# A VectorE division queued behind the activation of the tile at which it is emitted

## The chip, the cores and the metric

The kernel runs on one core of one Trainium2 chip. Its time is the device time of one execution in microseconds (us); lower is better. Three runs of the kernel before the change took 780.65 to 781.32 us, with a median of 781.09 us. The profile is one execution of the same program, recorded by the hardware profiler.

## The reference

Three stages follow one another (batch 4, 8 heads, 768 positions, head size 64; 3072 tokens of 512 values):

```
scores = [ q.k within 16 positions , q.(max of k over each 32) + log 32 ] / sqrt(64)
a      = exp(scores - rowmax);  a = a / (sum(a) + 1e-9)
x      = a @ [v ; mean of v over each 32]          # attention, reshaped to 3072 x 512
h      = x @ w_in;  x = (h * cos(h)) @ w_out       # 512 -> 2048 -> 512
logits = x @ phi;  d = softmax over tokens;  c = softmax over the 32 slots
out    = c @ experts(d.T @ x)                      # 8 experts, 4 slots each
```

The line that matters here is the division `a / (sum(a) + 1e-9)`.

## The kernel before

**Middle stage.** The 3072 tokens are taken in 6 blocks of 512, and the 2048 hidden values in 16 slices of 128, so there are 96 tiles `s`, 16 to a block. For each tile TensorE makes `h` with 12 matmuls of 512 columns (`mm1`: L384, L385, L388; the operands are split in a high and a low part). VectorE rounds in two steps (`act1`: L402, L403), ScalarE takes the sine (L404), VectorE multiplies by `h` (`act2`: L409), ScalarE makes the high part (L412) and GpSimd the low one (L413). Two tiles later TensorE adds the product to four accumulators with 12 more matmuls (`mm2`: L425, L426, L429). `h` has two PSUM buffers, so `mm1` of tile s + 2 needs that L409 of tile s is done. At the end of a block the accumulators are copied to `x` by VectorE (L448, two of them) and ScalarE (L446, two), and the next block's first `mm2` waits for these copies. The weights of each tile are split by ScalarE (L372) and GpSimd (L373).

**Attention inside the tiles.** The attention of a later block runs between these tiles. It is cut into 24 groups `g`, and from group 8 on two groups make a pair that shares one tile `S` of 128 x 16 x 120 values. Per pair and in this order: scores on TensorE (L286), scale and mask (L290), row maximum (L298) and its subtraction (L302) on VectorE, one exponential for both groups on ScalarE (L307), then for each group the row sum (L312), and the division in three VectorE instructions (`att_norm`: L326 adds 1e-9 and a factor on 128 x 8, L328 takes the reciprocal, L329 multiplies 128 x 960 values). TensorE then transposes the group in two halves (`att_C`: L336) and multiplies by v (`att_D`: L354). There are 8 pairs from group 8 on; the first is groups 8 and 9, the last groups 22 and 23.

**What sets the order.** The calls are entered under half tiles (`at2`) and emitted by `fire` while the tile loop runs: position 0 of a tile lies between its `act1` and its `act2`. The division of the first group of a pair is emitted at half tile n, that of the second at n + 4, so two tiles later: at tiles 17 and 19 for the first pair, 25 and 27 for the next, and so on in steps of 8 up to 73 and 75. The first transposition of a group is emitted one tile after its division. From tile 17 on (`MAN0`) the queues of TensorE and of the DMA-issuing engine hold their work in the order of emission. VectorE, ScalarE and GpSimd are ordered by a planner (`schedule_with_timeline_sim`), which takes what is ready first in its own simulated time; it may run an instruction well ahead of where it was emitted.

Of the kernel before, what the change touches and what calls it, by code (L numbers as in the profile page):

```python
# [15 lines left out]
ALU = mybir.AluOpType  # L16
# [58 lines left out]
MAGIC = 12582912.0  # L75
# [3 lines left out]
def body(ctx: ExitStack, tc: tile.TileContext, q0, qk, kT, vn, vx, w, phi, ex, cst, out):  # L79
    nc = tc.nc  # L80
# [241 lines left out]
    def att_norm(g, eng=None):  # L322

        d = grp[g]
        sm = d["sm"]
        nc.vector.tensor_scalar(out=sm, in0=sm, scalar1=1e-9, scalar2=W_SCALE * TWO_PI, op0=ALU.add, op1=ALU.mult)  # L326
        rs = stat.tile([128, 8], F32, name=f"rs{g}", tag="rs")
        nc.vector.reciprocal(out=rs, in_=sm)  # L328
        (eng or nc.vector).tensor_tensor(out=d["S"], in0=d["S"],  # L329
                                         in1=rs.unsqueeze(2).to_broadcast([128, 8, KC]), op=ALU.mult)  # L330
# [47 lines left out]
    def mm1(s):  # L378
# [9 lines left out]
            nc.tensor.matmul(h, lo[:, c], xh[s // NF][:, t, :], start=False, stop=t == 3)  # L388
        hps[s] = h

    def act1(s):
        h = hps[s]
        a = ring.tile([128, TB], F32, name=f"a{s}", tag="a")
        if s < NACT:
            nc.scalar.activation(a, h, AF.Identity, bias=magic)
            nc.vector.scalar_tensor_tensor(out=a, in0=a, scalar=MAGIC, in1=h, op0=ALU.subtract, op1=ALU.subtract)
            if s < NABS:
                nc.scalar.activation(a, a, AF.Abs)
            else:
                nc.vector.tensor_single_scalar(out=a.bitcast(I32), in_=a.bitcast(I32), scalar=0x7FFFFFFF, op=ALU.bitwise_and)  # L400
        else:
            nc.vector.tensor_scalar(out=a, in0=h, scalar1=0.25, scalar2=MAGIC, op0=ALU.add, op1=ALU.add)  # L402
            nc.vector.scalar_tensor_tensor(out=a, in0=a, scalar=MAGIC, in1=h, op0=ALU.subtract, op1=ALU.subtract)  # L403
        nc.scalar.activation(a, a, AF.Sin, bias=halfpi, scale=-TWO_PI)  # L404
        gs[s] = a

# [131 lines left out]
    def at(s, pos, fn, *a):  # L538
        bg.setdefault((s, pos), []).append((fn, a))

    def at2(h, fn, *a):
        at(max(h, 0) // 2, max(h, 0) % 2, fn, *a)
# [51 lines left out]
    for token in PRE.split():  # L594
        n = token.lstrip("FfIMNASPKQWBVGXmksevtdcwa")
        todo[token[:len(token) - len(n)]](int(n or 0))


    for g in range(4, 24):
        h0 = HF[g // 2 % 2] + 2 * NF * (g // 4 - 1) if g > 7 else HB[g // 2 % 2]  # L600
        h = h0 + OA * (g % 2)
        n = h0 + ON + DN * (g % 2)
        if g < 8:
            if g > 5:
                at2(h - OV, load_v, g)
                at2(h - OV + 1, load_vs, g)
                at2(h - OK, att_K, g)
            c = n + OC
            at2(c + OD, att_D, g)
        else:  # L610
            v = n - 14 + OD2
            at2(v + 1, load_v, g)
            at2(v + 2, load_vs, g)
            at2(h - OK, att_K, g)
            c = n + OC2
            at2(n + OD2, att_D, g)
        at2(h, att_A, g)
        if g < 8:
            at2(h + 1, att_max, g, True)
            at2(h0 + OX, att_exps, g)  # L620
        else:
            at2(h + 1, att_max, g)
            at2(h + 1, att_sub, g)
            if g % 2:
                at2(h0 + OX, att_exp, g // 2)
            at2(h0 + OS + 2 * (g % 2), att_sum, g)
        at2(n, att_norm, g)
        at2(c, att_C, g, 0)
        at2(c + 1, att_C, g, 1)
        if g + 2 < 24:  # L630
            at2(h0 + OQ if g < 8 else h + 1, load_qk, g + 2)
# [48 lines left out]
    for s in range(NSLOT + LAG):  # L680
        if MAN is not None and s == MAN0:
            guard = tc.manual_schedule(engines=MAN)
            guard.__enter__()
        if s < NSLOT:
            mm1(s)
        if s + 1 < NSLOT:
            split_w((s + 1) % NF, 0, nc.vector if s + 1 < NF else None)
        if 0 <= s - LAG + 1 < NSLOT:
            split_w((s - LAG + 1) % NF, 1)
        if s < NSLOT:  # L690
            act1(s)
        fire(s, 0)
        if s < NSLOT:
            act2(s)
        if s >= LAG:
            mm2(s - LAG)
            if (s - LAG) % NF == NF - 1:
                last = [x2_out(t) for t in range(4)][3]
        fire(s, 1)
        fire(s, 2)  # L700
        if s - LAG >= NSLOT - NF:
            grab(wres, f"w{s - LAG - (NSLOT - NF)}")
# [66 lines left out]
    for k in range(4):  # L769
# [3 lines left out]
                                    in1=rz.unsqueeze(1).to_broadcast([128, 4, 32]), op=ALU.mult)  # L773
# [170 lines left out]
```

## Time and profile before

| | |
|---|---|
| timed, median of 3 | 781.09 us (780.65 to 781.32) |
| profiled execution, first to last instruction (span) | 778.9 us |
| its own time outside the span | not listed; the span is 2.19 us under the median of the timed runs |
| TensorE matmul busy | 740.2 us (95%) |
| VectorE busy | 473.6 us (61%) |
| ScalarE busy | 433.4 us (56%) |
| GpSimd busy | 428.6 us (55%) |
| chain that ended last, by engine | PE 63%, DVE 13%, ACT 12%, DMA 6% |

PE is TensorE, PEld its weight load, DVE VectorE, ACT ScalarE, POOL GpSimd, SP the engine that issues DMAs. Times are us from the start of the span. In a row of the timeline the first number is the start, the second the duration; `x4` means four such instructions in a row; what stands in brackets is how long the engine had been idle and what ended that idle time. The modelled ends of matmuls overlap the next start, so the distance between starts tells more of TensorE's pace than the duration.

### The profile page before, as it was taken

How to read it: one execution, taken by the hardware profiler on the slowest of the kernel's cores; microseconds unless marked ns; L12 is line 12 of the kernel's file. 1: busy time of each engine (PE TensorE's matmuls, PEld its weight loads, DVE VectorE, ACT ScalarE, POOL GpSimd, SP SyncE). 2: the span in 40 equal slices, each digit the busy share in tenths (PEclk: the TensorE clock that was granted, in tenths of full speed). 3: DMA queues.
4: the chain of work that ended last, by engine and by line, in shares of the span. 5: the costliest groups of instructions: out<-in, count | busy, mean ns of one | idle time of the engine just before them, and what ended most of it. 6: DMA issues, size and time to landing. Idle time of an engine off the chain costs nothing.

```text
span 778.9 us, 13853 instructions
## 1 busy us (share of the span) xinstructions
PE 740.2 (95%) x5517; PEld 573.5 (74%) x5517; DVE 473.6 (61%) x686; ACT 433.4 (56%) x786; POOL 428.6 (55%) x302
## 2 busy tenths in 40 slices
PE   9977799998999999998999999999999999999994
PEld 7866678776877787776787777778768888786453
DVE  4578896767477576576575684774773444433523
ACT  4979868636465455574465555464554455443222
POOL 2555884365557657556566566665576665752000
PEclk9997999999999999999999999999999999999998
DMA  9988753121120331311211211301101922328978
GB/s 331 396 264 331 271 164 113 42 97 59 48 95 1 100 105 29 121 68 41 87 44 33 72 40 33 111 0 35 33 1 56 392 93 82 109 81 299 371 306 268
DMA packets 35585, 101.69 MB, mean 131 GB/s; under 512 B 3393, under 2 KB 13889, under 8 KB 33473
## 3 DMA queue, kind: packets, MB, share of 16 engines
q1 hardware_dynamic: 35520, 100.81, 36.8%
q8 instruction: 43, 0.70, 0.4%
q14 instruction: 22, 0.17, 0.1%
HBM read 92.54 MB, written 6.29 MB: 127 GB/s over the span
## 4 chain that ended last, share of the span: by engine, by line
PE 63%; DVE 13%; ACT 12%; DMA 6%; issue 4%; SPq 0%; ACTq 0%; DVEq 0%
PE acc L425 8%; PE h L384 8%; PE acc L426 8%; PE h L385 8%; PE acc L429 7%; PE h L388 7%; PE av L354 3%; DVE S L329 2%; DMA qk<-in_qk_dram 2%; PE yp L842 2%; DMA kr<-in_kT_dram 2%; PE sc L286 2%; PE hp L809 2%; ACT a L404 2%; DVE a L403 2%
## 5 line engine op out<-in xcount | busy, mean ns | idle before, releaser
L373 POOL TENSOR_TENSOR wol<-w,woh 128x512 fp32r<-128x512 f32 x96 | 143.9, 1500 | 115.0 <-ACT woh L372 115.0
L413 POOL TENSOR_TENSOR gl<-a,gh 128x512 fp32r<-128x512 f32 x96 | 129.0, 1343 | 83.8 <-ACT gh L412 78.3
L384 PE MATMUL h<-xh,wih 128*128 128x512 f32 x384 | 156.4, 407 | 6.7 <-DVE a L409 6.6
L425 PE MATMUL acc<-woh,gh 128*128 128x512 f32 x384 | 157.4, 410 | 3.5 <-DVE x L448 3.5
L385 PE MATMUL h<-xl,wih 128*128 128x512 f32 x384 | 152.2, 396 | 0.0
L426 PE MATMUL acc<-wol,gh 128*128 128x512 f32 x384 | 152.1, 397 | 0.0
L373 POOL TENSOR_TENSOR wil<-w,wih 128x512 fp32r<-128x512 f32 x81 | 113.9, 1406 | 42.8 <-PE h L388 24.2
L402 DVE TENSOR_SCALAR a<-h 128x512 f32<-128x512 f32 x96 | 65.9, 686 | 115.8 <-PE h L388 110.7
L404 ACT ACTIVATE a<-a,halfpi 128x512 f32<-128x512 f32 x96 | 69.4, 724 | 115.7 <-DVE a L403 115.4
L388 PE MATMUL h<-xh,wil 128*128 128x512 f32 x384 | 104.9, 395 | 0.0
L429 PE MATMUL acc<-woh,gl 128*128 128x512 f32 x384 | 104.6, 393 | 0.0
L409 DVE TENSOR_TENSOR a<-h,a 128x512 f32<-128x512 f32 x96 | 66.1, 689 | 57.0 <-ACT a L404 56.9
L425 PEld LDWEIGHTS acc<-woh,gh 128*128 128x128 f32 x384 | 72.4, 188 | 28.6 <-issue 11.8
L384 PEld LDWEIGHTS h<-xh,wih 128*128 128x128 f32 x384 | 72.7, 189 | 24.6 <-DVE a L409 8.4
L372 ACT CAST wih<-w 128x512 fp32r<-128x512 f32 x96 | 59.2, 617 | 47.2 <-PE h L385 46.4
L388 PEld LDWEIGHTS h<-xh,wil 128*128 128x128 f32 x384 | 72.5, 189 | 16.3 <-issue 0.2
L429 PEld LDWEIGHTS acc<-woh,gl 128*128 128x128 f32 x384 | 72.1, 189 | 16.4 <-issue 0.6
L385 PEld LDWEIGHTS h<-xl,wih 128*128 128x128 f32 x384 | 72.8, 190 | 15.2 <-issue 0.3
L426 PEld LDWEIGHTS acc<-wol,gh 128*128 128x128 f32 x384 | 72.6, 189 | 14.6 <-issue 0.6
L412 ACT CAST gh<-a 128x512 fp32r<-128x512 f32 x96 | 59.3, 619 | 32.8 <-DVE a L409 32.8
L372 ACT CAST woh<-w 128x512 fp32r<-128x512 f32 x96 | 59.1, 616 | 21.7 <-PE acc L429 20.8
L403 DVE SCALAR_TENSOR_TENSOR a<-a,h 128x512 f32<-128x512 f32 x96 | 65.5, 683 | 2.1
(137 smaller groups left out, 945.8 us busy)
## 6 DMA issues: line engine op xcount, KB each, us to landing
ex<-in_ex_dram SPq DMA_DIRECT2D x64, 512.0 KB
raw<-in_w_dram SPq DMA_DIRECT2D x16, 1024.0 KB
qk<-in_qk_dram SPq DMA_DIRECT2D x20, 736.0 KB
v<-in_vx_dram SPq DMA_DIRECT2D x24, 512.0 KB
kr<-in_kT_dram SPq DMA_DIRECT2D x16, 384.0 KB
vb<-in_vn_dram SPq DMA_DIRECT2D x12, 512.0 KB
out_dram<-o SPq DMA_DIRECT2D x12, 512.0 KB
v<-vs SPq DMA_DIRECT2D x40, 48.0 KB
```

The lines of the kernel that those rows point to most:

```text
L372: nc.scalar.copy(hi, W[f][:, part, :])
L373: (eng or nc.gpsimd).tensor_tensor(out=lo, in0=W[f][:, part, :], in1=hi, op=ALU.subtract)
L384: nc.tensor.matmul(h, hi[:, c], xh[s // NF][:, t, :], start=t == 0, stop=False)
L385: nc.tensor.matmul(h, hi[:, c], xl[s // NF][:, t, :], start=False, stop=False)
L388: nc.tensor.matmul(h, lo[:, c], xh[s // NF][:, t, :], start=False, stop=t == 3)
L403: nc.vector.scalar_tensor_tensor(out=a, in0=a, scalar=MAGIC, in1=h, op0=ALU.subtract, op1=ALU.subtract)
L404: nc.scalar.activation(a, a, AF.Sin, bias=halfpi, scale=-TWO_PI)
L409: nc.vector.tensor_tensor(out=a, in0=h, in1=a, op=ALU.mult)
L413: nc.gpsimd.tensor_tensor(out=gl, in0=a, in1=gh, op=ALU.subtract)
L425: nc.tensor.matmul(acc[t], gh[:, c], hi, start=f == 0, stop=False)
L426: nc.tensor.matmul(acc[t], gh[:, c], lo, start=False, stop=False)
L429: nc.tensor.matmul(acc[t], gl[:, c], hi, start=False, stop=f == NF - 1)
```

## The change

A call of `act1` now keeps its L403 instruction, and the division of the second group of a pair, from group 9 on, is emitted inside `tc.issue_after(...)` of the latest one. That adds, to each VectorE instruction traced in the block, an edge by which it stands behind that L403 in VectorE's queue. No instruction, buffer or semaphore's meaning is added or taken away; the division of the first group and of groups below 8 is emitted as before.

```diff
+    turn_dve = {}
+
     def act1(s):
...
-            nc.vector.scalar_tensor_tensor(out=a, in0=a, scalar=MAGIC, in1=h, op0=ALU.subtract, op1=ALU.subtract)
+            turn_dve["a"] = nc.vector.scalar_tensor_tensor(out=a, in0=a, scalar=MAGIC, in1=h, op0=ALU.subtract, op1=ALU.subtract)
...
+    def later(g):
+        with tc.issue_after(turn_dve["a"].ins):
+            att_norm(g)
...
-        at2(n, att_norm, g)
+        at2(n, att_norm if g < 8 or g % 2 == 0 else later, g)
```

## Rows read from the trace of the kernel before

**Rows 1.** Windows: stretch, length, busy per engine, then granted clock, DMA share, GB/s
```profile
176.00:600.00 424.00, 411.95 (x2850) 324.06 (x2850) 278.05 (x393) 238.04 (x386) 259.51 (x183) 1.00 0.17 54
600.00:690.00 90.00, 90.00 (x449) 72.43 (x446) 37.96 (x62) 44.22 (x74) 58.54 (x46) 1.00 0.43 158
```

**Rows 2.** Waits of PE from 176 to 600: who for whom, us, times, longest
```profile
PE h L384 <- DVE a L409: 4.8, 4, 1.4
PE acc L425 <- DVE x L448: 3.5, 3, 1.3
PE vs L184 <- DVE d L501: 1.8, 1, 1.8
PE tr L336 <- ACT aT L342: 0.2, 1, 0.2
```

**Rows 3.** Timeline of DVE around the pair of groups 10 and 11
```profile
241.39 4.25 DVE L329 TENSOR_TENSOR S<-S,rs 128x960 f32<-128x960 f32 x2
245.57 0.68 DVE L402 TENSOR_SCALAR a<-h 128x512 f32<-128x512 f32 x1
...
247.83 0.69 DVE L409 TENSOR_TENSOR a<-h,a 128x512 f32<-128x512 f32 x1 [0.79 <-ACT a L404]
```

**Rows 4.** Timeline of PE, where it waits for DVE in three pairs
```profile
183.35 0.50 PE L384 MATMUL h<-xh,wih 128*128 128x512 f32 x1 [1.38 <-DVE a L409]
...
248.58 0.50 PE L384 MATMUL h<-xh,wih 128*128 128x512 f32 x1 [1.15 <-DVE a L409]
...
297.12 0.60 PE L336 MATMUL tr<-ident,S 128*120 128x128 f32 x4
...
298.98 0.47 PE L425 MATMUL acc<-woh,gh 128*128 128x512 f32 x1 [1.26 <-DVE x L448]
```

**Rows 5.** Timeline of PE without such a wait, tile 28
```profile
258.52 1.08 PE L388 MATMUL h<-xh,wil 128*128 128x512 f32 x4
259.43 0.60 PE L336 MATMUL tr<-ident,S 128*120 128x128 f32 x4
259.79 0.48 PE L425 MATMUL acc<-woh,gh 128*128 128x512 f32 x1
```

**Rows 6.** Timeline of PE at the first transposition of group 18
```profile
463.78 1.08 PE L388 MATMUL h<-xh,wil 128*128 128x512 f32 x4
...
464.98 0.63 PE L336 MATMUL tr<-ident,S 128*120 128x128 f32 x4
```

**Rows 7.** Timeline of DVE around the pair of groups 12 and 13
```profile
295.71 1.66 DVE L329 TENSOR_TENSOR S<-S,rs 128x960 f32<-128x960 f32 x1
297.29 0.94 DVE L170 TENSOR_REDUCE ks<-kr 128x24 f32<-128x768 f32 x1
298.15 1.27 DVE L448 TENSOR_SCALAR x<-acc 128x512 f32<-128x512 f32 x2
```

**Rows 8.** The division's lines on DVE: count, ns min/median/max, first and last start
```profile
L326 DVE TENSOR_SCALAR sm<-sm x24: 154/164/1285, 18.0 to 570.7; 128x8 f32<-128x8 f32 x24
...
L328 DVE RECIPROCAL rs<-sm x24: 144/202/205, 18.2 to 572.0; 128x8 f32<-128x8 f32 x24
...
L329 DVE TENSOR_TENSOR S<-S,rs x20: 1150/2079/2254, 62.1 to 574.2; 128x960 f32<-128x960 f32 x20
```

**Rows 9.** Timeline of POOL beside the division of groups 10 and 11
```profile
242.43 2.21 POOL L373 TENSOR_TENSOR wil<-w,wih 128x512 fp32r<-128x512 f32 x1
```

**Rows 10.** Timeline of DVE at tile 27, where group 11's division is emitted
```profile
252.45 0.69 DVE L403 SCALAR_TENSOR_TENSOR a<-a,h 128x512 f32<-128x512 f32 x1
...
257.31 0.69 DVE L363 TENSOR_TENSOR xl<-av,xh 128x512 fp32r<-128x512 f32 x1 [2.63 <-ACT xh L362]
259.71 0.69 DVE L402 TENSOR_SCALAR a<-h 128x512 f32<-128x512 f32 x1 [1.71 <-PE h L388]
```

**Rows 11.** Timeline of DVE and then PE at tiles 67 and 68, group 21
```profile
528.35 0.68 DVE L403 SCALAR_TENSOR_TENSOR a<-a,h 128x512 f32<-128x512 f32 x1
...
534.58 0.60 PE L336 MATMUL tr<-ident,S 128*120 128x128 f32 x4
```

## The prediction

> **What bounds the kernel now.** I read four views. First the page's busy shares: TensorE's is by far the largest, VectorE's the next. Then the windows, to see whether that share hides idle places: from 600 to 690 us TensorE is busy 90.00 of 90.00 us, while in the stretch with the interleaved attention, 176 to 600 us, it is busy 411.95 of 424 us; the granted clock is 1.00, the higher of its two levels, 2.4 GHz, in both [rows 1]. So 12 us of that stretch are idle, and TensorE is at a full clock even where it never pauses. Third, the list of TensorE's waits in that stretch, which names what ends them: four waits for the multiplication L409, three for the accumulator copies L448, one for L501 and one for an ACT copy [rows 2]. The only other one of size is that of a transposition for its own group's division, in the first pair; it is the first group's, so it stays. Last, the timeline of VectorE ahead of one such wait: before it, both divisions of the pair run back to back, 4.25 us for the two L329, and the rounding L402 of the next tile starts only behind them, at 245.57; its product L409 starts at 247.83 and TensorE's `mm1` two tiles on starts at 248.58 after idling 1.15 us [rows 3, 4]. The second division, that of group 11, is emitted at tile 27, but by the count of L402 the one at 245.57 is tile 25's: the planner ran it more than a tile early, in front of work that TensorE was about to need.
>
> **The place that is left.** In seven of the eight pairs TensorE has a wait of this kind just behind the two divisions. Each is worth the distance between starts over what it is undisturbed. Transposition to the next L425 takes 0.36 us undisturbed (259.43 to 259.79) [rows 5]; in the pair of groups 12 and 13 it takes 1.86 us (297.12 to 298.98), so 1.50 us are lost where the listed wait is 1.26 [rows 4]. The listed wait is thus some 0.25 us short, as modelled ends overlap the next start. The same two starts in the other pairs with such a wait give 0.23 to 0.25 on top. Sum: three waits for L409 (of the four, the one at 183.35, 1.38 us, lies ahead of any division and stays [rows 4]) 4.8 - 1.4 = 3.4; three for L448 3.5; L501 1.8; the ACT copy 0.2; together 8.9 us [rows 2]. Six times 0.25 more is 1.5, and 0.2 for the last two: 10.6 us. In two pairs the first group's own transposition is late as well: L388 to L336 takes 1.20 us (463.78 to 464.98) [rows 6] where 0.91 is normal (258.52 to 259.43) [rows 5], 0.29 lost, twice: 0.6 us. In all 11.2 us.
>
> Does the wait vanish, or does the next one show? In the pair of groups 10 and 11 the second division holds VectorE for its L326, here the longest of them with 1.28 us, its reciprocal (0.2) [rows 8] and about half of the 4.25 us of L329 [rows 3]. Without these 3.5 us L409 starts at about 244.3 and ends at 245.0, while TensorE, not held, could begin `mm1` at 248.58 - 1.4 = 247.2: 2.2 us to spare. ScalarE's and GpSimd's work for tile 27 hangs on the same L403 and moves with it. In the pair of groups 12 and 13 the second L329 is 1.66 us, and behind it come the key maximum L170, 0.94 us from 297.29, and at 298.15 the accumulator copies [rows 7]; without it they start at 296.5, and the first is done at 297.1, when TensorE, held by nothing, would want it at 297.12 + 0.36 = 297.5 [rows 4, 5]; the second copy is done at 297.8 and wanted some four matmuls later (0.91 / 4 = 0.23 us each [rows 5]), at 298.4. That is the tightest, with 0.4 us to spare. So I take the whole 11.2 us, and keep for the range the case in which these three pairs stay late.
>
> **What the change adds.** No instruction is added. Per pair, three VectorE instructions (L326, L328, L329) now stand behind L403 of the tile of emission, 8 times. Their price at the new place is bounded by rows: from 0.16 + 0.20 + 1.15 = 1.5 us (each usual or at its fastest [rows 8]) to 1.28 + 0.20 + 2.25 = 3.7 us (each at its longest). I take 2.5 us, since at most one or two GpSimd operations lie near. What covers it at tile 27: L403 ends at 253.14, and VectorE is then idle for 2.63 and 1.71 us up to L402 of the next tile at 259.71 [rows 10], 4.3 us in all against at most 3.7. What queues behind it: at tile 27 the copy into `sacc`, and L409 of the same tile, which comes some 0.8 us after L403 where the queue is short [rows 3] and is now late by 1.7 us (up to 2.9); behind L409 ScalarE's and GpSimd's split of that tile. They are wanted by `mm1` of tile 29 and by `mm2` of tile 27, both a whole tile and more later. Who waits for the division itself: the first transposition of its group, emitted one tile on. It starts 259.43 - 253.14 = 6.3 us after L403 at tile 27 [rows 5, 10], and 534.58 - 529.03 = 5.55 us after it at tile 67 [rows 11], the shortest of the eight. Against 3.7 us nothing is late: cost 0, and if the cover were gone it would be 8 times the excess. The loads of v, qk and the weights hang on transpositions and scores, not on the division, so the DMA queue sees nothing but earlier times. ScalarE and GpSimd keep their instructions.
>
> Of the fastest and the slowest L329, 1.15 and 2.25 us, the slow ones run beside GpSimd's split, which then takes 2.21 us itself [rows 8, 9]. The Trainium skill, "SBUF — State Buffer", section "SBUF: two separate sides", has it that a VectorE operation with two SBUF inputs and a GpSimd operation take a shared port pair as an exclusive lock, one waiting for the whole of the other. The trace agrees. By that rule the new place is not free: each of the two locking instructions can wait for one GpSimd operation there, which is the upper end above and no more, so the sum by the rule is the same 11.2 us.
>
> **Sum.** Span 778.9 - 11.2 = 767.7 us. The timed median is 2.19 us over the span, which I leave as it is: 769.9 us, 1.4% less. Behind 600 us TensorE has no slack either [rows 1], so the earlier end of the loop passes to the end.
>
> **Rivals.** First, the next wait takes over in part. In the three pairs where a block ends, the copies L448 have little to spare: in the pair worked out above 0.4 us, and only if the load that L170 reads has landed 1.7 us earlier than it was used (L170 starts with no idle time ahead of it, so the rows don't tell). The planner may also set other ready work ahead of the copies. Then 3.5 + 0.75 = 4.2 us stay, and the gain is 7.0: 774.1 us. For it speaks the small margin, and that the planner orders VectorE, ScalarE and GpSimd anew; against it, that TensorE's order is fixed and the planner already had these copies next after the division but for L170 [rows 7].
>
> Second, nothing changes (within 0.2%): the planner fills the freed place with other work that was not wanted yet, so the same rounding is late again, or TensorE is not the bound and later idle time eats the gain: 781 us. Against it: nothing else of VectorE's is ready then, and TensorE's starts are an even 0.23 us apart wherever it does not wait [rows 5]. The Trainium skill, "Perfetto Trace Analysis", section "Identifying the Most-Contended Engine", warns that a matmul busy share is no measure of closeness to the bound and points to the weight loads, here 324 of 424 us or 76%. By that one could doubt the bound; the even distance of starts decides for it.
>
> Third, slower: the edge sets only an earliest place, and the planner puts the second division behind still more of VectorE's queue, up to L363, which itself waits for ScalarE till 257.31 and ends at 258.0 [rows 10]. The division then ends 1.5 to 3.7 us later, at 259.5 to 261.7, and its transposition, due at 259.43, holds TensorE for 0.1 to 2.3 us in each of eight pairs. The point from which it decides is 11.2 / 8 = 1.4 us a pair; at the far end, 2.3, it is 8 x 2.3 - 11.2 = 7 us slower, at 1.8 some 3 us: 784 us. For it: in the trace the planner does not keep the order of emission. Against it: it has moved these divisions forward, never back, and the sums are long ready.
>
> **How the numbers follow.** Forecast 0.77; partial gain 0.11; no change 0.04; slower 0.08. What can be told from no change is about 0.2%, 1.6 us. Faster is forecast and first rival, 0.88; same 0.04; slower 0.08. The forecast's own range is 768 to 772: down by the wait and the late transposition of the first pair (183.35 [rows 4]), of which a reordering may take some, up by a few new small waits. To hold 8 in 10 it reaches over the partial gain: 768.0 to 776.0.
>
> **What would show it.** In the trace after: a single L329 ahead of L402 of tiles 25, 33, 41 and so on, and the other right behind L403 of tiles 27, 35, 43; TensorE's list from 176 to 600 us without L448 and L501, with one wait for L409; TensorE busy within 4 us of the whole length of that stretch; transpositions of odd groups without a wait. The prediction is wrong if waits for L448 stay (first rival), if the transposition of odd groups waits for L329 (third), or if the two L329 still stand together.

## The result, and the profile after

| | before | after |
|---|---|---|
| timed, median of 4 | 780.87 us (780.19 to 781.32) | 768.51 us (767.90 to 769.20) |
| profiled span | 778.9 us | 767.2 us |
| ratio after / before | | 0.9839 [0.9819, 0.9859] |
| start of tile 17's first L384 to the start of the last `mm2` matmul | 536.71 us | 524.80 us |

The kernel is 1.6% faster; 769.9 us were forecast. The last line of the table, called the stretch from here on, is read from starts in the timeline of TensorE. It holds all tiles at which the pairs' divisions are emitted. It changed by -11.91 us; the span changed by -11.7. What lies behind the stretch lasts 65.9 to 66.6 us in every run of this study, while the start-up ahead of it differs from one execution to the next: tile 17 begins at 175.2 to 178.5 us, in one execution of an experiment at 181.76. A second execution of the changed kernel has a stretch of 524.87 us, 0.07 from the first. Differences of a microsecond are therefore read in the stretch, and the timed medians are given beside it.

In the kernel after, lines from L402 on have moved down by two: rounding L404 and L405, sine L406, product L411, splits L414 and L415, `mm2` L427, L428 and L431, accumulator copies L450. L503 and L520 (L501 and L518 before) are two small copies for the last stage, of `d` and into `sacc`.

The page of after, busy time by engine and the chain that ended last:

```profile
PE 738.0 (96%) x5517; PEld 574.7 (75%) x5517; DVE 464.9 (61%) x686; ACT 432.9 (56%) x786; POOL 423.8 (55%) x302
...
PE 87%; ACT 7%; DVE 2%; DMA 2%; issue 1%; DVEq 0%; ACTq 0%; SPq 0%
```

TensorE's share of the chain rose from 63 to 87%, VectorE's fell from 13 to 2%: behind the first pair VectorE no longer holds up a matmul of the middle stage. The busy shares themselves say little of that (TensorE 95 to 96%).

Windows of after, the stretches that answer to [rows 1], the second moved by the 11.7 us that the end moved:

```profile
176.00:600.00 424.00, 421.17 (x2916) 334.08 (x2915) 274.96 (x400) 242.67 (x394) 262.34 (x189) 1.00 0.18 62
588.30:678.30 90.00, 90.00 (x448) 72.40 (x445) 37.96 (x62) 44.15 (x75) 58.57 (x46) 1.00 0.43 158
```

Idle time of TensorE fell from 12.05 to 2.83 us, with the granted clock at 1.00 in both. Of what waits it is made says the list of TensorE's waits in after from 176 to 600 us, which answers to [rows 2]:

```profile
PE tr L336 <- DVE S L329: 1.6, 1, 1.6
PE h L384 <- DVE a L411: 1.3, 1, 1.3
```

The waits for the accumulator copies, for L501 and for the ACT copy are gone, and of the four for the product one is left. Both that are left stand in the first pair, as before.

Timeline of VectorE in after around the pair of groups 10 and 11 (start, duration), which answers to [rows 3, 10]:

```profile
240.19 2.04 DVE L329 TENSOR_TENSOR S<-S,rs 128x960 f32<-128x960 f32 x1
242.15 0.68 DVE L404 TENSOR_SCALAR a<-h 128x512 f32<-128x512 f32 x1
...
244.47 0.69 DVE L411 TENSOR_TENSOR a<-h,a 128x512 f32<-128x512 f32 x1 [0.85 <-ACT a L406]
...
250.94 0.69 DVE L405 SCALAR_TENSOR_TENSOR a<-a,h 128x512 f32<-128x512 f32 x1
251.55 1.07 DVE L326 TENSOR_SCALAR sm<-sm 128x8 f32<-128x8 f32 x1
252.53 0.68 DVE L520 COPY sacc<-sp 128x512 f32<-128x512 f32 x1
253.13 0.18 DVE L328 RECIPROCAL rs<-sm 128x8 f32<-128x8 f32 x1
253.24 0.63 DVE L411 TENSOR_TENSOR a<-h,a 128x512 f32<-128x512 f32 x1
253.80 1.14 DVE L329 TENSOR_TENSOR S<-S,rs 128x960 f32<-128x960 f32 x1
```

One L329 stands ahead of tile 25's rounding, the other behind L405 of tile 27. The planner did not run the moved division in one piece: it put the `sacc` copy and the product L411 between its parts. The division ends at 254.94, 3.3 us after L405. Over the eight pairs it ends 1.5 to 3.6 us after L405 and 2.75 to 4.4 us ahead of its transposition.

Timeline of TensorE in after: the `mm1` that was late in [rows 4], the moved group's own transposition, and the transposition and first `mm2` at the block end:

```profile
246.74 0.60 PE L336 MATMUL tr<-ident,S 128*120 128x128 f32 x4
247.10 0.48 PE L384 MATMUL h<-xh,wih 128*128 128x512 f32 x1
...
257.96 0.60 PE L336 MATMUL tr<-ident,S 128*120 128x128 f32 x4
...
295.65 0.60 PE L336 MATMUL tr<-ident,S 128*120 128x128 f32 x4
296.00 0.48 PE L427 MATMUL acc<-woh,gh 128*128 128x512 f32 x1
```

No row has an idle time in brackets, and what follows the first and the last transposition starts 0.36 and 0.35 us later, the undisturbed distance of [rows 5]. The product that `mm1` needs is done at 244.47 + 0.69 = 245.16, 1.9 us early. The moved division is done 3.0 us before its transposition at 257.96.

Timeline of VectorE in after at that block end, which answers to [rows 7]:

```profile
292.11 1.66 DVE L329 TENSOR_TENSOR S<-S,rs 128x960 f32<-128x960 f32 x1
293.69 0.68 DVE L405 SCALAR_TENSOR_TENSOR a<-a,h 128x512 f32<-128x512 f32 x1
294.29 0.94 DVE L170 TENSOR_REDUCE ks<-kr 128x24 f32<-128x768 f32 x1
295.15 1.27 DVE L450 TENSOR_SCALAR x<-acc 128x512 f32<-128x512 f32 x2
```

Half of the last row's 1.27 us is the first copy: it is done at 295.8 and wanted at 296.00.

The distances between the same instructions of TensorE before and after, from tile to tile, give what each pair of groups gave back:

| pair | 8/9 | 10/11 | 12/13 | 14/15 | 16/17 | 18/19 | 20/21 | 22/23 | sum |
|---|---|---|---|---|---|---|---|---|---|
| us less | 0.15 | 1.47 | 1.50 | 2.23 | 1.54 | 1.71 | 1.59 | 1.72 | 11.91 |

### The profile page after: what moved, and what is told of

Read it like the earlier page. It is cut to its first block, busy times and chain, and to the rows that moved or that the text cites. A ratio compares the mean times of both kernels' runs of the same rounds, so it can differ in the third digit from the quotient of the medians.

```text
span 767.2 us, 13871 instructions
## 1 busy us (share of the span) xinstructions
PE 738.0 (96%) x5517; PEld 574.7 (75%) x5517; DVE 464.9 (61%) x686; ACT 432.9 (56%) x786; POOL 423.8 (55%) x302
## 4 chain that ended last, share of the span: by engine, by line
PE 87%; ACT 7%; DVE 2%; DMA 2%; issue 1%; DVEq 0%; ACTq 0%; SPq 0%
PE acc L427 12%; PE acc L428 11%; PE acc L431 11%; PE h L384 11%; PE h L385 11%; PE h L388 11%; PE av L354 3%; PE sc L286 3%; PE tr L336 2%; PE yp L848 2%; PE hp L815 2%; PE xt L455 1%; PE warmth L570 1%; ACT w L129 1%; ACT cv L130 1%
## 5 line engine op out<-in xcount | busy, mean ns | idle before, releaser
L373 POOL TENSOR_TENSOR wol<-w,woh 128x512 fp32r<-128x512 f32 x96 | 141.2, 1471 | 111.2 <-ACT woh L372 111.2
L415 POOL TENSOR_TENSOR gl<-a,gh 128x512 fp32r<-128x512 f32 x96 | 132.5, 1381 | 90.7 <-ACT gh L414 85.2
L384 PE MATMUL h<-xh,wih 128*128 128x512 f32 x384 | 156.4, 407 | 3.1 <-DVE a L411 3.1
L427 PE MATMUL acc<-woh,gh 128*128 128x512 f32 x384 | 157.3, 410 | 0.0
L428 PE MATMUL acc<-wol,gh 128*128 128x512 f32 x384 | 152.1, 397 | 0.0
L385 PE MATMUL h<-xl,wih 128*128 128x512 f32 x384 | 151.9, 396 | 0.0
L404 DVE TENSOR_SCALAR a<-h 128x512 f32<-128x512 f32 x96 | 65.8, 686 | 126.0 <-PE h L388 117.4
L406 ACT ACTIVATE a<-a,halfpi 128x512 f32<-128x512 f32 x96 | 69.4, 724 | 103.2 <-DVE a L405 97.9
L373 POOL TENSOR_TENSOR wil<-w,wih 128x512 fp32r<-128x512 f32 x81 | 108.4, 1338 | 33.6 <-PE h L388 20.5
L431 PE MATMUL acc<-woh,gl 128*128 128x512 f32 x384 | 105.1, 394 | 0.0
L411 DVE TENSOR_TENSOR a<-h,a 128x512 f32<-128x512 f32 x96 | 65.8, 686 | 53.7 <-ACT a L406 53.5
L427 PEld LDWEIGHTS acc<-woh,gh 128*128 128x128 f32 x384 | 72.4, 188 | 23.9 <-issue 8.9
L384 PEld LDWEIGHTS h<-xh,wih 128*128 128x128 f32 x384 | 72.8, 190 | 20.1 <-DVE a L411 3.9
L431 PEld LDWEIGHTS acc<-woh,gl 128*128 128x128 f32 x384 | 72.3, 189 | 16.5 <-issue 0.6
L385 PEld LDWEIGHTS h<-xl,wih 128*128 128x128 f32 x384 | 72.9, 190 | 15.2 <-issue 0.2
L428 PEld LDWEIGHTS acc<-wol,gh 128*128 128x128 f32 x384 | 72.7, 190 | 14.6 <-issue 0.6
L414 ACT CAST gh<-a 128x512 fp32r<-128x512 f32 x96 | 59.3, 619 | 36.4 <-DVE a L411 36.3
L405 DVE SCALAR_TENSOR_TENSOR a<-a,h 128x512 f32<-128x512 f32 x96 | 65.5, 683 | 2.2
```

Source lines behind the costliest of these rows:

```text
L373: (eng or nc.gpsimd).tensor_tensor(out=lo, in0=W[f][:, part, :], in1=hi, op=ALU.subtract)
L384: nc.tensor.matmul(h, hi[:, c], xh[s // NF][:, t, :], start=t == 0, stop=False)
L385: nc.tensor.matmul(h, hi[:, c], xl[s // NF][:, t, :], start=False, stop=False)
L411: nc.vector.tensor_tensor(out=a, in0=h, in1=a, op=ALU.mult)
L415: nc.gpsimd.tensor_tensor(out=gl, in0=a, in1=gh, op=ALU.subtract)
L427: nc.tensor.matmul(acc[t], gh[:, c], hi, start=f == 0, stop=False)
```

## The experiments

The theory is that the gain is TensorE's idle time behind the double division and nothing else, pair by pair. The rivals are: that the edge makes the planner lay the queues better in general; that the gain comes from products that no longer run beside GpSimd's splits; that the exact place matters; and that any VectorE time at the new place would cost. The "before" of each ratio ran on the same chip. Durations called "the stretch" come from the profiled execution.

**Half of the change, twice.** The edge on three groups only, those of the block ends, and on the other four:

```diff
-        at2(n, att_norm if g < 8 or g % 2 == 0 else later, g)
+        at2(n, later if g in (13, 17, 21) else att_norm, g)       # block ends
+        at2(n, later if g in (11, 15, 19, 23) else att_norm, g)   # other pairs
```

> Only the second groups of the three pairs at a block's end (groups 13, 17, 21) are queued behind the activation; the other five divisions stay where the kernel before has them. Theory W (the gain is the TensorE idle time behind the double division, pair by pair): only the three waits for L448 go, 1.5 + 1.4 + 1.5 = 4.4 us, so about 776.5 us, and the waits for L409 and L501 in the other pairs stay in the trace. Rival P (one edge makes the planner lay all queues anew, and that is the gain): the gain is not made of parts, so the time is near that of the whole change, 768.5 us, or of none, 781 us.

> Only the second groups of the other four pairs (11, 15, 19, 23) are queued behind the activation. Theory W: the waits for L409 and L501 and the late transpositions behind them go, 1.4 + 2.2 + 1.6 + 1.7 = 6.9 us, so about 774 us; the three waits for L448 stay. With the run of the block ends the two gains add up to that of the whole change within 1.5 us. Rival P: they do not add up.

Block ends: 776.62 us against 781.43, ratio 0.9958 [0.9933, 0.9984]; its runs spread from 774.81 to 782.13, so the stretch is what counts: 4.59 us shorter. Other pairs: 773.06 us, ratio 0.9890 [0.9874, 0.9907]; stretch 7.33 us shorter. TensorE's waits from 176 to 600 us with the edge at the block ends only:

```profile
PE h L384 <- DVE a L411: 4.7, 4, 1.4
PE vs L184 <- DVE d L503: 1.8, 1, 1.8
...
```

and with the edge at the others only:

```profile
PE acc L427 <- DVE x L450: 3.3, 3, 1.3
...
```

Each half takes away its own entries of [rows 2] and leaves the other's; what else the lists hold is the first pair's and, in the first, the ACT copy's 0.2. 4.59 + 7.33 = 11.92 us, where the whole change gave 11.91: the gains belong to the single pairs, and they add.

**No second product, no edge.** The kernel before, with the product of the second group of each pair left out:

```diff
-        (eng or nc.vector).tensor_tensor(out=d["S"], in0=d["S"],
-                                         in1=rs.unsqueeze(2).to_broadcast([128, 8, KC]), op=ALU.mult)
+        if g < 8 or g % 2 == 0:
+            (eng or nc.vector).tensor_tensor(out=d["S"], in0=d["S"],
+                                             in1=rs.unsqueeze(2).to_broadcast([128, 8, KC]), op=ALU.mult)
```

> The kernel before without any edge, with the L329 of the second groups from 9 on left out (these groups stay undivided, so the output is not the reference's). Theory W: what delays TensorE is the time that stands ahead of the rounding step or the copies, and 1.66 to 2.25 us of it are gone where 1.4 to 1.9 us were lost, so the waits go as with the change, 768 to 770 us. Rival P (the edge and the planner's new order give the gain): about 781 us, the waits stay. Rival G (fewer collisions of VectorE and GpSimd give the gain): clearly below the change, 766 us or less, since 8 products with their collisions are gone altogether.

768.69 us against 781.51, ratio 0.9834 [0.9817, 0.9852]; stretch 525.44, 0.64 above that of the change. The order of before, without an edge, is as good as the change once the second product is out of the way. So the gain is the second product's time ahead of the tile's own work, and not a better lay-out by the planner. It is no better than the change either, though eight products and their collisions with GpSimd are gone. Its list of TensorE's waits holds the same two as that of after, 1.6 and 1.2 us.

Of the 0.64 us that it lacks, nearly 0.6 are the two late transpositions of first groups of which [rows 6] show one. Here they are still late, by 0.28 us each, because the second group's long L326 still stands ahead of the first group's product. The timeline of VectorE and then of TensorE in this kernel, whose lines are one lower from L329 on:

```profile
454.15 1.28 DVE L326 TENSOR_SCALAR sm<-sm 128x8 f32<-128x8 f32 x1
...
456.62 1.08 PE L389 MATMUL h<-xh,wil 128*128 128x512 f32 x4
457.82 0.63 PE L337 MATMUL tr<-ident,S 128*120 128x128 f32 x4
```

The distance is 1.20 us as in [rows 6]; in after the same two stand at 457.05 and 457.96, 0.91 apart.

**A tile earlier.** The second division is emitted one tile earlier, behind that tile's activation:

```diff
+        at2(n if g < 8 or g % 2 == 0 else n - 2, att_norm if g < 8 or g % 2 == 0 else later, g)
```

> The second division is emitted one tile earlier than in the change, behind the activation of tile s - 1. There VectorE is idle for 2.0 to 4.1 us in the trace of the change before the next rounding step, against 1.5 to 3.7 us for the division. Theory W: cost 0, the same as the change within 1 us (about 768.5 us), TensorE's waits as in the change. Rival R (the place behind the activation of tile s itself is what helps, for instance by the port shared with GpSimd): 771 us or more.

768.79 us against 781.77, ratio 0.9823 [0.9775, 0.9870]; stretch 524.80 us, that of the change to the last digit. One tile does not matter. It settles the rival of the collisions too. The durations of L329 on VectorE (ns, least, median, most) in after, and then in this kernel:

```profile
L329 DVE TENSOR_TENSOR S<-S,rs x20: 1141/1158/2103, 61.6 to 574.6; 128x960 f32<-128x960 f32 x20
```

```profile
L329 DVE TENSOR_TENSOR S<-S,rs x20: 1148/1968/2116, 60.7 to 567.4; 128x960 f32<-128x960 f32 x20
```

The change brought the median down from 2079 ns [rows 8] to 1158, because at the new place none of the eight moved products starts beside a running GpSimd split (they take 1.14 to 1.16 us). A tile earlier seven of the eight do (1.91 to 1.98 us), the median is back at 1968, and the time is the same.

**Two tiles earlier in the queue.** Emitted three half tiles earlier than in the change, which puts it two activations further ahead in VectorE's queue:

```diff
+        at2(n if g < 8 or g % 2 == 0 else n - 3, att_norm if g < 8 or g % 2 == 0 else later, g)
```

> The second division is emitted half a tile less than two tiles earlier, behind the activation of tile s - 2, the tile before whose rounding the kernel before had it. Theory W: in the four pairs away from a block's end the multiplication of that tile (L411 there) ends at 245.8 to 248 us in the first of them, where TensorE wants it at 247.2, so 0 to 0.8 us are lost in each; at the three block ends the accumulator copies stand partly behind it, 0 to 1 us each. Together 0 to 6 us on the change: 768.5 to 774.5, I take 770.5 us. Rival R: as the kernel before, 779 us or more, since both divisions are close together again.

775.92 us against 781.77, ratio 0.9908 [0.9878, 0.9938]; stretch 5.78 us above the change. That is dearer than the 768.5 to 774.5 us expected: the block ends lost up to 1.8 us, not up to 1, and the first pair had no term. The four pairs away from a block end lose 0, 0.40, 0 and 0 us; the three at a block end lose 0.53, 1.80 and 1.68, the first pair 1.37. Waits of TensorE from 176 to 640 us:

```profile
PE tr L336 <- DVE S L329: 2.8, 1, 2.8
PE acc L427 <- DVE x L450: 2.7, 5, 0.9
...
```

and the timeline of VectorE at the second of these block ends:

```profile
404.93 1.21 DVE L326 TENSOR_SCALAR sm<-sm 128x8 f32<-128x8 f32 x1
...
406.30 0.64 DVE L450 TENSOR_SCALAR x<-acc 128x512 f32<-128x512 f32 x1
406.85 1.15 DVE L329 TENSOR_TENSOR S<-S,rs 128x960 f32<-128x960 f32 x1
407.92 0.68 DVE L450 TENSOR_SCALAR x<-acc 128x512 f32<-128x512 f32 x1
```

Here the division lands among the accumulator copies, and L326 and L329 push them back; this is the first rival of the prediction, at another place. In the first pair group 9's L326 stands ahead of group 8's product, whose transposition waits 2.8 us and not 1.6. So the place matters by what stands behind it, and the copies with their small margin are where it shows most, with 4.0 of the 5.8 us.

**A tile later, and both divisions behind the activation.** First the second division one tile later than in the change; then, at the change's place, the first group's division behind its tile's activation as well:

```diff
+        at2(n if g < 8 or g % 2 == 0 else n + 2, att_norm if g < 8 or g % 2 == 0 else later, g)   # a tile later
+        at2(n, att_norm if g < 8 else later, g)                                                   # both
```

> The second division is emitted one tile later, behind L403's counterpart of tile s + 1, so that it ends after TensorE has reached its transposition. Theory W with the cover of 5.5 us: in each of eight pairs TensorE waits from the end of that tile's mm1 to the end of the division, 0.7 + 0.7 + 0.1 us for the two rounding steps and 1.5 to 3.7 us for the division, 3.0 to 5.2 us, that is 24 to 41 us on top of 768.5: 793 to 810 us, with eight waits of the transposition for L329. Rival P (only the spacing of the two divisions counts, not the place): about 768.5 us.

> The first group's division too is queued behind the activation of the tile at which it is emitted. Theory W: the first division is wanted by its transposition less than 2 us after it ends in the changed kernel, so behind L403's counterpart it is late by 0 to 2 us in most of seven pairs: 771 to 778 us, slower than the change, with waits of the first group's transposition for L329. Rival P (order of emission is better as such): the same as the change or faster, 767 to 768.5 us.

A tile later: 811.16 us against 781.43, ratio 1.0384 [1.0358, 1.0410]; stretch 43.2 us above the change. Both: 779.37 us, ratio 0.9979 [0.9958, 1.0001]; stretch 11.6 us above the change. They lie 1.2 and 1.4 us above their expected ranges, in which the clock had no term. Waits of TensorE from 170 to 650 us a tile later:

```profile
PE tr L336 <- DVE S L329: 27.0, 9, 3.2
...
```

and for both, from 176 to 620 us:

```profile
PE tr L336 <- DVE S L329: 9.4, 8, 2.2
...
```

This is the wait of the third rival, the transposition that waits for its own division. Besides the first pair's 1.6 us there are eight waits of 3.18 us in the one, and seven more, of 0.51 to 2.16 us, in the other. In the one a start that waits comes 3.58 us after the matmul ahead of it instead of 0.23: 8 x 3.35 = 26.8 us. The other 16 us are TensorE's clock. The timeline of TensorE at one such wait in that kernel, and two windows of the same place (busy times per engine, then granted clock, DMA share and GB/s):

```profile
265.38 1.08 PE L336 MATMUL tr<-ident,S 128*120 128x128 f32 x4 [3.18 <-DVE S L329]
```

```profile
264.30:271.10 6.80, 5.72 (x16) 4.69 (x17) 1.53 (x2) 1.44 (x3) 1.28 (x1) 0.50 0.04 11
271.20:280.00 8.80, 8.80 (x95) 6.89 (x94) 5.19 (x7) 3.73 (x7) 3.98 (x4) 1.00 0.36 125
```

From late in this wait on the granted clock is 0.50, the lower level of 1.2 GHz, and starts of matmuls are 0.43 us apart instead of 0.23. The low clock lasts 3.41 us at five of the waits and 6.83 us at three, 37.5 us in all, of which 3.5 still lie within the waits. At these distances the other 34.0 lose 34.0 x (1 - 0.23 / 0.43) = 15.8 us. With the waits that makes 42.6, where 43.2 were measured.

In the kernel with both, the seven waits cost 9.0 us from start to start, and the clock fell for 3.41 us behind the longest of them, some 1.5 us. About 0.9 us more are lost at the block ends of pairs 16/17 and 20/21, where the accumulator copies stand behind the late division.

**More VectorE time at the new place.** Behind each moved division one further product of the same shape by ones, then three:

```diff
     def later(g):
         with tc.issue_after(turn_dve["a"].ins):
             att_norm(g)
+            for _ in range(1):       # 3 in the second kernel
+                nc.vector.tensor_tensor(out=grp[g]["S"], in0=grp[g]["S"],
+                                        in1=ones[:, 0:8].unsqueeze(2).to_broadcast([128, 8, KC]), op=ALU.mult)
```

> The change, with one more 128 x 960 product (by ones) behind each second division, 8 in all, before its transposition. In the trace of the change the second L329 ends 3.0 us before its transposition starts (254.94 to 257.96 in the pair of groups 10 and 11). Theory W: the added product takes 1.15 to 2.25 us, all within the cover: 0 on the change, 768.5 us within 1. Rival R2 (VectorE's or GpSimd's time as such counts, also where TensorE does not wait): 8 x 1.15 to 2.25 = 9 to 18 us more, 778 to 786 us.

> The change, with three more such products behind each second division, 24 in all. Theory W: the cover of 3.0 us is used up; three products and the work of VectorE that the planner puts between them end 0.5 to 3 us after TensorE reaches the transposition: 8 x 0.5 to 3 = 4 to 24 us on the change, 773 to 793, I take 780 us, with eight waits of the transposition for VectorE. If single waits come near 3 us the granted clock will fall behind them as in the run with the division a tile later (there 0.50 for 3.4 or 6.8 us after waits of 3.2 us). Rival R2: 24 x 1.15 to 2.25 = 28 to 54 us more, 796 us or more.

One more: 768.78 us against 781.77, ratio 0.9819 [0.9775, 0.9863]; stretch 524.88 us, 0.08 above the change. The price of the moved division is zero with room to spare, as predicted. Three more: 802.31 us, ratio 1.0244 [1.0195, 1.0293]; stretch 31.6 us above the change, where about 12 were expected. This is a miss: the time lies above the expected range and within that of rival R2, by which VectorE's time counts as such. What speaks against R2 is the one product more, which costs nothing, and the place of the loss: the eight waits make 24.5 us of it from start to start, and the clock the rest. Waits of TensorE with three more, from 176 to 640 us, and the added products (L605) at tile 27 with the transposition that they make late:

```profile
PE tr L336 <- DVE S L605: 23.2, 8, 3.8
...
```

```profile
258.49 4.31 DVE L605 TENSOR_TENSOR S<-S,ones 128x960 f32<-128x960 f32 x2
...
263.32 1.62 DVE L605 TENSOR_TENSOR S<-S,ones 128x960 f32<-128x960 f32 x1
...
265.08 0.62 PE L336 MATMUL tr<-ident,S 128*120 128x128 f32 x4 [3.48 <-DVE S L605]
```

The expectation was too low for two reasons: a product takes up to 2.15 us here (the first two of the rows 4.31 together) and not 1.15, and the clock fell at three of the eight waits, for 17.1 us in all, some 7 us lost.

**The two waits that are left.** Both stand in the first pair. In the first of two kernels VectorE's accumulator copies are issued behind the latest L329, so that they no longer stand ahead of the first group's product; in the second the exponential of that pair is also issued behind the sine of tile 16, so that it doesn't hold ScalarE in front of it:

```diff
+        turn_dve["n"] = (eng or nc.vector).tensor_tensor(out=d["S"], in0=d["S"],
...
+            with tc.issue_after(turn_dve["n"].ins):
+                nc.vector.tensor_scalar_mul(x2[:, t, :], acc[t], TWO_PI / W_SCALE)
...
+    def exp_first(pair):                                   # second kernel only
+        with tc.issue_after(turn_dve["sin"].ins):
+            att_exp(pair)
```

> The change, and at a block's end VectorE's two accumulator copies are queued behind the latest L329. This alters VectorE's order in the first pair alone, where the trace of the change still has a wait of 1.6 us for the division of group 8, with the two copies (2 x 0.6 us) between its L326 and its L328. Theory W: group 8's division ends 1.2 us earlier, and TensorE's wait there shrinks from 1.6 to about 0.4 us; the copies are done before TensorE wants them. 1.2 us less than the change, 767.3 us. Rival P (the planner's order elsewhere shifts and gives or takes as much): no change or more, and the wait for L329 keeps its 1.6 us.

> As the run before, and the exponential of the first pair is queued on ScalarE behind the sine of tile 16. Theory W: the product of tile 16 is ready at 178 instead of 183.3 us, so the wait of 1.3 to 1.5 us for it goes; the sums and group 8's division start 1.3 us later, so that its transposition, reached 1.4 us earlier, waits about 1 us. Together 2 us less than the change, 766.5 us. Rival P: no less than the run before, since the later exponential gives back what the sine wins.

> The changed kernel once more on the same chip as the two runs beside it, as their base: 768.5 us within 1 by every theory; only the stretch before tile 17 should differ between executions.

Against 781.51 us on this chip the kernel after took 768.93 us, ratio 0.9839 [0.9822, 0.9856], with a stretch of 524.87; with the copies behind it 768.27 us, ratio 0.9827 [0.9810, 0.9844], stretch 523.50; with the exponential too 768.22 us, ratio 0.9832 [0.9812, 0.9852], stretch 523.60. Waits of TensorE from 176 to 640 us, with the copies moved (in both kernels `mm1` is one line lower, at L385, and the product one higher, at L410):

```profile
PE h L385 <- DVE a L410: 1.2, 1, 1.2
PE tr L336 <- DVE S L329: 0.3, 1, 0.3
```

and with both moved:

```profile
PE tr L336 <- DVE S L329: 1.8, 1, 1.8
```

The first does what was expected: 1.3 us of the transposition's wait are gone and come out of the stretch. The timed medians cannot tell so little; only the trace shows it. The second misses. The product's wait of 1.2 us is gone, so TensorE reaches the transposition 1.4 us earlier, but the division ends no earlier: 10.17 us after the start of tile 17, where it was 10.10 with the copies alone. The row sums follow the exponential, which is 1.35 us later, and the division's product takes 1.97 us there instead of 1.51; what makes up for it is a short L326 (0.42 us instead of 1.09) and L410, which no longer stands in between. The transposition can't start before this chain of exponential, sum and division has ended, so what the edge takes from one wait goes to the other.

## Why the prediction was right, step by step

- **What bounds.** Right. TensorE's starts set the time wherever it doesn't wait. With the second product left out of the order of before, or with another product behind the moved division, the stretch stays within 0.7 us of the change's.
- **The sum of 11.2 us.** The stretch gave 11.91. The waits themselves were sized well: the waits of [rows 4], plus the 0.25 us of overlap, give 1.40 us for pair 10/11 and 1.51 for 12/13, and 1.47 and 1.50 were measured. The term that was too small is that of the losses no list shows. They were given 0.6 us, for two late transpositions. At pair 10/11 a third one is late, by 0.09 us. And at the block ends of pairs 16/17 and 20/21, 1.54 and 1.59 us came back where the listed wait and the overlap make 1.34 and 1.38. The timeline of TensorE in the kernel before, behind the first of these waits:

```profile
410.87 0.47 PE L425 MATMUL acc<-woh,gh 128*128 128x512 f32 x1 [1.09 <-DVE x L448]
...
411.64 0.40 PE L426 MATMUL acc<-wol,gh 128*128 128x512 f32 x1
411.98 0.50 PE L425 MATMUL acc<-woh,gh 128*128 128x512 f32 x1
412.31 0.40 PE L426 MATMUL acc<-wol,gh 128*128 128x512 f32 x1
```

Four matmuls on, the starts are 0.34 and 0.33 us apart instead of 0.23. The later L425 is the first on the accumulator of VectorE's second copy, which ends at 411.93, just ahead of that start at 411.98. So this is a second, small wait, which no list shows. It makes 0.2 us, and as much at 521.36. The first pair's product wait, which was to stay, fell from 1.38 to 1.25 us, and that pair gave 0.15; what is left is under 0.1.
- **What is late next.** Right in direction, with less room than worked out. The product at pair 10/11 is 1.9 us early, predicted 2.2: the rounding L404 came forward by 3.42 us (245.57 to 242.15) and not by 3.5, the product comes 0.06 later behind it, and TensorE wants it 0.1 earlier, at 247.10. The copies at pair 12/13 are 0.2 us early, predicted 0.4: the second product had held the queue for 1.58 us (295.71 to 297.29 in [rows 7]) and not for its 1.66, and the first one ends 0.05 us later, seen from the transposition. The load that L170 reads had landed, which the rows before could not tell.
- **The cost of the moved division.** Zero, as taken, though not for 2.5 us in one piece: at pair 10/11 it ends 3.3 us after L405 with a copy and a product between its parts, inside the 6.3 us to its transposition (251.63 to 257.96; as before). The shortest cover in after is 5.9 us, where 5.55 was predicted. One more product of 2.1 us at that place costs 0.08 us in the whole stretch, three cost 31.6: that brackets the cover.
- **The rivals.** The partial gain and the slower case are real mechanisms and did not occur at this place; two tiles earlier in the queue shows the one, a tile later the other. Of the clock the third rival's price, 8 x 2.3 us of waits at the far end, had nothing. The kernel a tile later, where the division is later still, has 26.8 us of waits and another 16 from the clock; whether waits of 2.3 us would have brought the clock down is open, as it fell at one of 2.16 us and stayed at others of 3.2.
- **From span to time.** 778.9 - 11.2 + 2.19 = 769.9 was forecast, the profiled execution of after took 769.20, and the median of four is 768.51. The first 0.7 us are the sum's. The last 0.7 are a difference between executions of one kernel, which the forecast could not know; in the traces such differences lie in the start-up ahead of the stretch.
- **The signs.** They are there: two waits of the first pair alone, 2.83 us of idle time, no odd group's transposition late. Only at the block end shown the first product stands between the two roundings and not ahead of both, where it also stood in the kernel before.

## What to carry to other kernels

In a queue that a planner orders, work that is ready but not yet wanted can stand ahead of work that the bounding engine needs next; an edge that says "not before this instruction" cost nothing here, as the queue has idle time between there and the consumer. Count both margins before placing it: here the place may move a tile earlier and still gives 524.80 us, but a tile later costs 43 us and two tiles earlier 5.8. And compare distances between starts with the undisturbed distance: the list of waits alone showed 8.9 of the 11.9 us.

## What the runs showed of the hardware that was not expected

**TensorE's clock can fall at a single wait.** In the kernel before, with waits of 0.2 to 1.8 us, the granted clock of the stretch stays at 1.00 [rows 1]. With the division a tile later it fell to 0.50 at each of the eight waits of 3.18 us. With three more products it fell at waits of 2.74, 3.75 and 3.72 us, not at 3.48, 3.16 and 3.17; with both divisions behind the activation, at one of 2.16 us. Windows of the kernel with three more products, at the waits of 3.75 and of 3.48 us:

```profile
491.86:498.69 6.83, 5.33 (x15) 4.40 (x16) 3.33 (x4) 1.82 (x3) 1.61 (x2) 0.50 0.03 7
265.00:272.00 7.00, 6.92 (x48) 5.63 (x52) 2.16 (x4) 3.63 (x6) 2.78 (x3) 1.00 0.01 2
```

So the length of the wait alone doesn't decide; what else does stays open. For a price, from these traces: the wait of 3.18 us at pair 10/11 of the kernel a tile later cost 6.0 us, that of 3.75 us in the windows above 6.4, and that of 2.16 us 3.9.

**Two engines on SBUF.** Over all traces here, 136 of the products L329 on VectorE start with no GpSimd instruction running, and each takes 1.14 to 1.16 us. The other 136 start while one runs, and each lasts as long as the rest of that instruction plus 1.01 to 1.02 us, 1.49 to 2.26 in all. The 128 x 8 instruction L326 takes 0.15 to 0.17 us by itself, but in after at 251.55 it takes 1.07 us, and it ends, at 252.62, just behind the split that was running:

```profile
251.29 1.30 POOL L373 TENSOR_TENSOR wil<-w,wih 128x512 fp32r<-128x512 f32 x1
```

The reciprocal stays at 0.14 to 0.21 us, beside a split too. The Trainium skill, "SBUF — State Buffer", section "SBUF: two separate sides", has it that a VectorE operation with two SBUF inputs or in a 2-port mode and a GpSimd operation take a shared port pair as an exclusive lock. The rows of L329 agree: a product that comes second waits for the whole rest of the GpSimd instruction. Those of L326, which has one SBUF input, agree if it runs in such a mode, which no trace names. For the time of this kernel it made no difference, as the run a tile earlier shows.
